# Attention by pair of heads ahead of two feed-forward nets: scores on quarters of the TensorE array, one transfer for queries and keys, softmax over several blocks at once, shared PSUM banks

## The chip, the cores and the metric

The kernel runs on one core of a Trainium2 chip. The metric is the device time of one execution in microseconds, the median of several runs. The profile is that of one execution, taken by the hardware profiler.

## What is computed

```
scores = scale * q @ k^T                                  # 4 batches, 8 heads, 576 tokens, 64 columns
mask_local   = (rel >= 0) & (rel < 32)                    # heads 0 to 3
mask_strided = (rel >= 0) & (pos_k % 32 == pos_q % 32)    # heads 4 to 7
attn = softmax(where(mask, scores, -1e9));  x = attn @ v  # x: [2304 tokens, 512]
h = x @ w_in;  x = (h * clip(h + 3, 0, 6) / 6) @ w_out    # 512 -> 2048 -> 512
h = x @ w_in2; out = (h * tanh(softplus(h))) @ w_out2
```

The weights come as doubles. Products of the two nets are made from split operands (a high and a low part of every number, three products in place of one); attention is in plain float32.

## The kernel before

**Attention.** A batch has four pairs of heads. A query sees few keys, so the 576 queries of a head are cut into nine blocks of 64, and a block is scored against the 96 keys (local heads) or 90 keys (strided heads) that it can see. A unit is three of the nine blocks of a pair, both heads: three units to a pair, twelve to a batch, 48 in all. `unit` scores a block of both heads with one product on the whole array: the stationary operand holds one head's 64 queries beside the other's, with zeros above and below, so that 128 rows of two heads come out (L415). VectorE scales, masks and takes the row's extremum with one fused instruction a block (L426), ScalarE takes the exponentials with their sums (L440, one instruction a block), VectorE adds 1e-9 and inverts (L450, L451), GpSimd multiplies (L444), TensorE transposes (L457), ScalarE or VectorE copies out of PSUM (L285, L287). `finish` makes the products with the values (L478), two units at a time from the second batch on, and splits the result into `xh` and `xl`.

**The nets.** Tokens go in five blocks (512, 512, 512, 256, 512). For each chunk of 128 of the 2048 hidden columns and each block there are four triples of products into the hidden chunk (from `xh`, `xl`) and four triples out of it (from `gh`, `gl`): L607, L608 and L609 are the three products of a triple. There are 1280 triples in all; a triple of 512 columns is three instructions of 128x512. A first-layer triple of the first token block needs the first batch's attention; later blocks need later batches.

**Order.** All engines' instructions are ordered ahead of time by a list planner (`Plan.run`) from estimated costs and due times, and stand in that order on the engines, which work strictly in it. SP issues all transfers, from one queue, in order as well. Numbers such as `UNIT` (an attention unit's time on TensorE), `START` and `EARLY_X` feed the planner, and `BANKS` says which of the eight PSUM banks each user may have. TensorE prints two records for every float32 product (it makes two passes) and one for each product of a triple and each transposition. In the first microseconds TensorE also multiplies zeros (L766) where it has nothing else to do.

Of the kernel before, what the change touches and what calls it, by code (L numbers as in the profile page):

```python
# [5 lines left out]
F32 = mybir.dt.float32  # L6
# [64 lines left out]
TWO_FROM = 1  # L71
#: Of mish: the seed a + b exp(-c w), and the step's square.
# [4 lines left out]
class Op:  # L77
    """Instructions of one engine that follow one another, what they wait for, and what they cost
    on the engines that could do them. VectorE and GpSimd read SBUF through a port that they share:
    lock names those engines on which the op holds it."""  # L80

    __slots__ = ("engine", "costs", "cost", "emit", "deps", "due", "bank", "frees", "start", "end", "left", "users", "rows", "lock")

    def __init__(self, costs, emit, deps, due, bank, frees, lock=""):
        self.engine, self.cost = min(costs.items(), key=lambda c: c[1])
        self.costs, self.emit, self.due = costs, emit, due
        self.deps = [d for d in deps if d is not None]
        self.bank, self.frees = bank, frees
# [13 lines left out]
class Plan:  # L102
    """Orders the instructions of all engines: each engine takes, of the instructions that can
    start first, the one that is due first."""

    #: From an instruction's end to the start of one that waits for it.
# [11 lines left out]
    def set_due(self):  # L118
        """What is due last before those that use it, back from the products."""
# [22 lines left out]
    def stream(self, t, op):  # L142
        """When TensorE, from t on, has done an op."""
# [10 lines left out]
    def fill(self, start, end, free_bank):  # L154
        """Products that nothing needs, on TensorE from start to end."""
# [14 lines left out]
    def run(self):  # L170
        """The instructions in the order of their starts."""
# [12 lines left out]
        while left:  # L184
            best = None
            for e, waiting in ready.items():
                for item in waiting:
                    r, op = item
                    if op.bank is not None and op.bank.n is None:
                        r = max(r, min(free_bank[n] for n in BANKS[op.bank.use]))  # L190
# [21 lines left out]
            if op.bank is not None and op.bank.n is None:  # L212
                op.bank.n = min(BANKS[op.bank.use], key=lambda n: free_bank[n])
                free_bank[op.bank.n] = 1e12
# [25 lines left out]
def copy_ns(n, psum=False):  # L240
    """Of a copy on either engine that may make it."""
# [3 lines left out]
def plain_ns(n):  # L245
    """Of two tensors' sum, difference or product."""
# [595 lines left out]
```

## Time and profile before

| | us |
|---|---|
| median of 3 runs | 907.26 (906.24 to 907.88) |
| profiled execution, span from first to last instruction | 909.7 |
| its own time apart from the span | not given; the span stands for it |
| TensorE busy | 901.1 (99%) |
| VectorE, ScalarE, GpSimd busy | 570.9, 543.7, 260.8 |
| bytes moved | 56.01 MB |

Read the page from its slices: a slice is 22.7 us, so attention (ended at 173.6 us on TensorE) fills the first seven or eight, and the rest is the nets.

### The profile page before, as it was taken

Reading aid. Unit: us, or ns where it says so; the run is one execution under the profiler, and the core shown is the slowest. Engines: PE = TensorE matmul, PEld = TensorE weight load, DVE = VectorE, ACT = ScalarE, POOL = GpSimd, SP = SyncE. Lnnn points to the kernel's source line nnn. Section 1 sums busy time; section 2 is a strip of 40 time slices with the busy share of each in tenths; the row PEclk is TensorE's granted clock in tenths of the full one; section 3 lists DMA queues with packets and bytes.
Section 4 is the critical chain, followed back from the end, with each engine's and each line's share of the span. In section 5 each row is a group of like instructions: output and inputs, shape, how many; then the busy total and the mean of one; then the engine's idle time right before and its main releaser. Section 6 shows DMA issues by size and latency. Waiting matters only on the chain.

```text
span 909.7 us, 13481 instructions
## 1 busy us (share of the span) xinstructions
PE 901.1 (99%) x4894; PEld 759.5 (83%) x4894; DVE 570.9 (63%) x1276; ACT 543.7 (60%) x1193; POOL 260.8 (29%) x240
## 2 busy tenths in 40 slices
PE   8999999999999999999999999999999999999998
PEld 8888888888888888888898888888888888888887
DVE  6787675588822258871237778646787787644454
ACT  6776867645322234332334878778887778666664
POOL 3223323232222222242443332222222222222222
PEclk9999999999999999999999999999999999999999
DMA  9944444022200002210002202100120110001111
GB/s 235 227 137 144 129 140 131 1 93 93 94 0 1 1 24 93 93 70 0 1 1 70 71 24 70 46 1 24 47 69 25 47 48 1 0 6 42 47 46 70
DMA packets 23146, 56.01 MB, mean 62 GB/s; under 512 B 2392, under 2 KB 9176, under 8 KB 23080
## 3 DMA queue, kind: packets, MB, share of 16 engines
q1 hardware_dynamic: 23080, 55.16, 19.7%
q8 instruction: 38, 0.62, 0.3%
q14 instruction: 28, 0.23, 0.1%
HBM read 50.43 MB, written 4.72 MB: 61 GB/s over the span
## 4 chain that ended last, share of the span: by engine, by line
PE 96%; DVE 1%; DMA 1%; SPq 1%; issue 0%; ACT 0%; DVEq 0%
PE bank L607 29%; PE bank L609 29%; PE bank L608 29%; PE bank L415 5%; PE bank L478 2%; PE bank L457 2%; DMA v<-in_qkv_dram 1%; SPq L380 0%; DVE e L426 0%; DVE wm L592 0%; SPq L388 0%; DVE y L739 0%; DVE sum L450 0%; SPq L383 0%; DVE t L618 0%
## 5 line engine op out<-in xcount | busy, mean ns | idle before, releaser
L701 POOL TENSOR_TENSOR gl<-t,gh 128x512 fp32r<-128x512 f32 (+1 forms) x160 | 197.8, 1237 | 534.6 <-ACT gh L285 485.4
L607 PE MATMUL bank<-xh,w 128*128 128x512 f32 (+1 forms) x640 | 240.0, 375 | 0.0
L607 PE MATMUL bank<-gh,w 128*128 128x512 f32 (+1 forms) x640 | 238.5, 373 | 0.0
L609 PE MATMUL bank<-xh,w 128*128 128x512 f32 (+1 forms) x640 | 237.5, 371 | 0.0
L608 PE MATMUL bank<-xl,w 128*128 128x512 f32 (+1 forms) x640 | 237.0, 370 | 0.0
L609 PE MATMUL bank<-gh,w 128*128 128x512 f32 (+1 forms) x640 | 237.0, 370 | 0.0
L608 PE MATMUL bank<-gl,w 128*128 128x512 f32 (+1 forms) x640 | 236.6, 370 | 0.0
L609 PEld LDWEIGHTS bank<-xh,w 128*128 128x128 f32 x640 | 120.7, 189 | 21.5
L607 PEld LDWEIGHTS bank<-xh,w 128*128 128x128 f32 x640 | 121.1, 189 | 20.4
L609 PEld LDWEIGHTS bank<-gh,w 128*128 128x128 f32 x640 | 120.4, 188 | 21.3
L608 PEld LDWEIGHTS bank<-xl,w 128*128 128x128 f32 x640 | 121.0, 189 | 20.5
L607 PEld LDWEIGHTS bank<-gh,w 128*128 128x128 f32 x640 | 120.6, 188 | 20.7
L608 PEld LDWEIGHTS bank<-gl,w 128*128 128x128 f32 x640 | 120.5, 188 | 20.6
L615 ACT ACTIVATE t<-bank 128x512 f32<-128x512 f32 (+1 forms) x80 | 44.4, 555 | 145.3 <-PE bank L609 143.6
L618 DVE SCALAR_TENSOR_TENSOR t<-t,bank 128x512 f32<-128x512 f32 (+1 forms) x80 | 50.6, 633 | 126.9 <-ACT t L615 126.6
L285 ACT CAST gh<-t 128x512 fp32r<-128x512 f32 (+1 forms) x160 | 91.3, 572 | 52.0 <-DVE t L618 27.6
L646 DVE SCALAR_TENSOR_TENSOR t<-t,seed 128x512 f32<-128x512 f32 (+1 forms) x80 | 60.8, 760 | 71.3 <-ACT seed L635 68.3
L651 DVE SCALAR_TENSOR_TENSOR t<-t,seed 128x512 f32<-128x512 f32 (+1 forms) x80 | 61.5, 770 | 48.0 <-ACT t L648 48.0
L639 ACT ACTIVATE t<-bank 128x512 f32<-128x512 f32 (+1 forms) x80 | 44.4, 555 | 60.4 <-PE bank L609 56.8
L648 ACT ACTIVATE t<-t,offset 128x512 f32<-128x512 f32 (+1 forms) x80 | 54.3, 679 | 23.2 <-DVE t L646 23.2
L739 DVE TENSOR_TENSOR y<-bank,y 128x512 f32<-128x512 f32 (+1 forms) x80 | 49.0, 634 | 21.8 <-PE bank L609 21.0
L444 POOL TENSOR_TENSOR e<-e,sum 128x288 f32<-128x288 f32 (+1 forms) x48 | 33.9, 711 | 89.9 <-DVE sum L451 47.2
(50 smaller groups left out, 1026.4 us busy)
## 6 DMA issues: line engine op xcount, KB each, us to landing
raw<-in_wts_dram SPq DMA_DIRECT2D x64, 512.0 KB, 3.5
k<-in_qkv_dram SPq DMA_DIRECT2D x15, 288.0 KB, 4.2
q<-in_qkv_dram SPq DMA_DIRECT2D x30, 144.0 KB, 4.4
out_dram<-y SPq DMA_DIRECT2D x16, 256.0 KB, 2.0
v<-in_qkv_dram SPq DMA_DIRECT2D x8, 432.0 KB, 4.7
v<-in_qkv_dram SPq DMA_DIRECT2D x7, 405.0 KB, 5.0
out_dram<-y SPq DMA_DIRECT2D x4, 128.0 KB, 1.8
mk_str<-in_masks_dram SPq DMA_DIRECT2D x1, 405.0 KB, 10.4
```

The costliest lines, as they stand in the source:

```text
L285: nc.scalar.copy(out, src)
L415: nc.tensor.matmul(banks[bank.n][:, j * LK:j * LK + nk], src.q[:, i].rearrange("p h (n j) -> p (h n) j", j=3)[:, :, j], src.k[:, k0:k0 + n ...
L607: nc.tensor.matmul(o, a[:, 1], high, start=first, stop=False)
L608: nc.tensor.matmul(o, a[:, 0], low, start=False, stop=False)
L609: nc.tensor.matmul(o, a[:, 0], high, start=False, stop=last)
L615: o = add("act", act_ns(n, True), lambda: nc.scalar.activation(t, h(), AF.Relu, bias=0.5, scale=1.0 / 6.0), [prod, free])
L618: lambda: nc.vector.scalar_tensor_tensor(t, t, 1.0, h(), ALU.min, ALU.mult), [o], frees=s.h,
L646: lambda: nc.vector.scalar_tensor_tensor(t, t, 4.0, seed(), ALU.add, ALU.mult), [o], lock=("dve",),
L648: o = add("act", act_ns(n), lambda: nc.scalar.activation(t, t, AF.Square, bias=offset, scale=scale), [o])
L651: lambda: nc.vector.scalar_tensor_tensor(t, t, more, seed(), ALU.add, ALU.mult), [o], lock=("dve",),
L701: lambda eng, gh=gh, gl=gl, t=t: engines[eng].tensor_tensor(gl, t, gh.bitcast(F32), ALU.subtract),
L739: lambda y=y, src=src: nc.vector.tensor_tensor(y(), src(), y(), ALU.add), [op, *before], due=due, frees=bank,
```

## The change

A unit becomes a whole pair. `attend` takes the place of `unit` and `finish`:

- **Scores.** A head's block is a product of its own on a quarter of the array: 64 rows of contraction (the head's columns) by 64 queries, 18 products to a pair, written to two banks, one for each head. No zeros stand beside the queries any more, so queries and keys come in one transfer of 128 x 1152 words, and values in one of all 128 rows (96 or 90 before).
- **Softmax.** Scores of a head are scaled and masked four blocks (two by two, one above the other) in one instruction, the ninth block in a second one; maxima are taken over four and over five block columns at once; sums, inverses and the multiplication go over four and five at once. The exponentials stay one instruction a block column, nine to a pair as before. The local mask is copied out four times on GpSimd at the start, the strided one comes in three smaller transfers.
- **Transpositions and values.** Nine transpositions to a pair, copied out in pieces of 4, 4 and 1; the values' products of eight blocks, then of the ninth.
- **Banks and plan.** Attention and the first layer's hidden chunks share banks 0 to 3; score, transposition and triple costs and the pace and due numbers of the planner are new.

```diff
-N_QKV, N_E, N_PT = 2, 4, 2
+N_QKV, N_E, N_PT = 2, 2, 2
...
-    "att": (2, 3),
+    "att": (0, 1, 2, 3),
...
-    "h0": (0, 1),
+    "h0": (0, 1, 2, 3),
...
-START, FIRST_PACE = 40000, 803
-UNIT = 800
+START, FIRST_PACE = 40000, 2409
+UNIT = 3000
...
-EARLY_W, EARLY_G, EARLY_X = 8224, 12000, 9101
+EARLY_W, EARLY_G, EARLY_X = 8224, 12000, 14000
...
+def mm3_ns(n):
+
+    return 3 * (n + 32) / 2.4
...
+        r.qk = add(
+            "dma", dma_ns(4 * P * 2 * S), lambda: nc.sync.dma_start(qk_t[n], qkv[b, p, :, :2 * S]), old.scores if old else [],
+        )
...
+        r.v_load = add(
+            "dma", dma_ns(4 * P * P * NB), lambda: nc.sync.dma_start(r.v, qkv[b, p, :, 2 * S:]), old.values if old else [],
+        )
...
+        def scores():
+            for n in range(NB):
+                for h in range(2):
+                    at = h if n == NB - 1 else n % 2
+                    nc.tensor.matmul(
+                        head(h)[at * QB:(at + 1) * QB, n // 2 * LK:n // 2 * LK + nk],
+                        src.q[h * D:(h + 1) * D, n // 3, :, n % 3],
+                        src.k[h * D:(h + 1) * D, first[n]:first[n] + nk],
+                        start=True,
+                        stop=True,
+                    )
...
+            nc.vector.scalar_tensor_tensor(
+                e[:, h * n:(h + 1) * n, :nk], x, 1.0 / INV_SCALE, mk_loc if local else mk_str[:, :n], ALU.mult, ALU.add
+            )
...
+        def most(s):
+            nc.vector.tensor_reduce(nmax[:, s], e[:, s, :nk], mybir.AxisListType.X, ALU.max, negate=True)
+
+        def exps(s):
+            for j in range(s.start, s.stop):
+                x = e[:, j, :nk]
+                nc.scalar.activation(x, x, AF.Exp, bias=nmax[:, j:j + 1], accum_out=total[:, j:j + 1])
...
+        s_op = add("pe", 36 * 44, scores, [src.qk, *e_free], bank=both)
...
-        s = add("pe", 640, scores, [*src.qk, e_free], bank=bank)
...
-                nc.tensor.matmul(
-                    banks[bank.n][:, j * LK:j * LK + nk],
-                    src.q[:, i].rearrange("p h (n j) -> p (h n) j", j=3)[:, :, j],
-                    src.k[:, k0:k0 + nk],
-                    start=True,
-                    stop=True,
-                )
```

**SP, the first transfers of the program** (`raw` are weights as doubles, `q`, `k`, `v` the operands of attention, `mk` and `mk_str` masks, `y` the memory in which the third pair's operands stand). Before:

```order
L558 DMA raw_91<-in_wts_dram 128x512
L383 DMA k_119<-in_qkv_dram 128x576
L380 DMA q_117<-in_qkv_dram 64x3x192 x2
L388 DMA mk<-in_masks_dram 128x320
L383 DMA k_120<-in_qkv_dram 128x576
L380 DMA q_118<-in_qkv_dram 64x3x192 x2
L392 DMA v_121<-in_qkv_dram 96x1152
L558 DMA raw_92<-in_wts_dram 128x512
L383 DMA y_77<-in_qkv_dram 128x576
L380 DMA y_77<-in_qkv_dram 64x3x192 x2
```

After:

```order
L392 DMA qk_118<-in_qkv_dram 128x1152
L372 DMA mk<-in_masks_dram 128x320
L392 DMA qk_119<-in_qkv_dram 128x1152
L392 DMA y_77<-in_qkv_dram 128x1152
L573 DMA raw_91<-in_wts_dram 128x512
L392 DMA qk_118<-in_qkv_dram 128x1152
L398 DMA v_120<-in_qkv_dram 128x1152
L380 DMA mk_str<-in_masks_dram 64x5x90
L380 DMA mk_str<-in_masks_dram 64x4x90
L380 DMA mk_str<-in_masks_dram 64x90
L398 DMA v_121<-in_qkv_dram 128x1152
L398 DMA y_78<-in_qkv_dram 128x1152
```

Four pairs' queries and keys and three pairs' values stand ahead of the second half chunk of weights now, where before that half chunk stood behind two pairs' queries and keys and one pair's values.

**TensorE, from the third product triple on**, where the start ends (`bank` are PSUM banks, `pt` the transposed weights of attention, `e` its weights, `w` decoded weights of the nets). Before, the part from the fourth pair's last units to the fourth and fifth triple:

```order
L607 MATMUL bank_62<-xh_71,w_79 128x512 [waits Activation_49]
L608 MATMUL bank_62<-xl_75,w_79 128x512 [waits DVE_49]
L609 MATMUL bank_62<-xh_71,w_79 128x512
L457 MATMUL bank_67<-mk,e_126 90x128 [waits Pool_49]
L457 MATMUL bank_67<-mk,e_126 90x128 x2
L478 MATMUL bank_63<-pt_135,v_121 64x64 [waits Activation_49]
L478 MATMUL bank_63<-pt_135,v_121 64x64 x5
L415 MATMUL bank_64<-k_119,q_117 128x96 [waits DMAHW3_49,DMAHW4_49,DMAHW2_49,DVE_49]
L415 MATMUL bank_64<-k_119,q_117 128x96 x2
L478 MATMUL bank_61<-pt_136,v_121 64x64 [waits Activation_49]
L478 MATMUL bank_61<-pt_136,v_121 64x64 x5
```

After, the fourth triple, and what stands between it and the fifth (18 rows of scores, of which the first two are shown):

```order
L623 MATMUL bank_63<-xl_76,w_79 128x512 [waits DVE_49]
L624 MATMUL bank_63<-xh_72,w_79 128x512
L479 MATMUL bank_62<-mk,e_122 96x128 [waits Pool_49]
L479 MATMUL bank_62<-mk,e_122 96x128 [waits Activation_49] x3
L479 MATMUL bank_61<-mk,e_122 96x128 [waits Pool_49]
L479 MATMUL bank_61<-mk,e_122 96x128 [waits Activation_49] x3
L479 MATMUL bank_63<-mk,e_122 96x128 [waits DVE_49]
L421 MATMUL bank_64<-qk_119 64x90 [waits DMAHW3_49,DVE_49]
L421 MATMUL bank_62<-qk_119 64x90 [waits Activation_49]
...
L498 MATMUL bank_61<-pt_128,v_121 64x64 [waits DMAHW2_49,Activation_49]
L498 MATMUL bank_61<-pt_128,v_121 64x64 x15
L622 MATMUL bank_66<-gh_103,w_80 128x512
```

Ahead of the fifth triple TensorE now waits for the queries and keys of the seventh pair (`qk_119`) and for the values of the fifth (`v_121`). Counted in the whole order, it has then 7 pairs of scores, 5 of transpositions and 5 of values behind it; before, it had 17 of 48 units of scores, 14 of transpositions and 12 of values. Behind the fifth triple there remain 31 units of scores, 34 of transpositions and 36 of values (in 24 groups) before, and 9 pairs of scores, 11 of transpositions and 11 of values (in 14 groups) now; 1276 triples either way.

## Rows read from the trace of the kernel before

**Rows 1.** The page, 40 slices of the span: TensorE's and the DMA engines' busy tenths.

```profile
PE   8999999999999999999999999999999999999998
...
DMA  9944444022200002210002202100120110001111
```

**Rows 2.** The page, the chain that ended last: shares by engine, then by line.

```profile
PE 96%; DVE 1%; DMA 1%; SPq 1%; issue 0%; ACT 0%; DVEq 0%
PE bank L607 29%; PE bank L609 29%; PE bank L608 29%; PE bank L415 5%; PE bank L478 2%; PE bank L457 2%; DMA v<-in_qkv_dram 1%; SPq L380 0%; DVE e L426 0%; DVE wm L592 0%; SPq L388 0%; DVE y L739 0%; DVE sum L450 0%; SPq L383 0%; DVE t L618 0%
```

**Rows 3.** Windows: length; busy of PE, PEld, DVE, ACT, POOL; clock; DMA share; GB/s.

```profile
0.00:12.00 12.00, 10.20 (x54) 9.94 (x55) 5.99 (x32) 6.02 (x21) 4.31 (x11) 1.00 0.83 247
12.00:24.00 12.00, 10.53 (x109) 9.95 (x108) 9.13 (x53) 8.55 (x37) 3.92 (x6) 1.00 1.07 220
24.00:36.00 12.00, 12.00 (x129) 10.88 (x129) 10.60 (x60) 9.63 (x41) 2.83 (x5) 1.00 1.03 234
36.00:46.00 10.00, 8.76 (x60) 7.52 (x59) 5.89 (x34) 6.80 (x29) 2.55 (x4) 0.75 0.74 211
46.00:174.00 128.00, 127.46 (x1000) 106.31 (x999) 86.88 (x361) 90.28 (x302) 39.34 (x45) 0.99 0.42 121
174.00:905.00 731.00, 731.00 (x3544) 613.98 (x3543) 450.94 (x736) 422.45 (x767) 207.84 (x170) 1.00 0.12 40
...
41.00:47.70 6.70, 6.70 (x34) 5.66 (x34) 4.18 (x21) 4.21 (x16) 0.86 (x2) 0.50 0.50 148
```

**Rows 4.** The chain cut to 46 to 174 us, shares by line.

```profile
by line: PE bank L415 25.0%; PE bank L607 16.5%; PE bank L609 15.3%; PE bank L608 15.0%; PE bank L478 10.9%; PE bank L457 9.2%; DVE e L426 1.2%; DVE t L618 1.0%; DVE sum L450 1.0%; issue 0.9%; DVE wm L592 0.9%; DVE wa L569 0.6%; DVE wa L578
```

**Rows 5.** The chain in order of time, pieces: start us, us, what (records).

```profile
32.19 2.06 PE bank L415 x12
34.26 0.85 PE bank L478 x24
...
96.08 0.33 PE bank L457 x3
97.90 0.23 PE bank L608
99.06 0.50 PE bank L478 x12
101.74 1.01 PE bank L415 x6
```

**Rows 6.** Groups by line and shape, weight loads: xcount, busy us, mean ns, idle.

```profile
L415 PEld LDWEIGHTS bank<-k,q 128*128 128x128 f32 x270 | 51.0, 262 | 5.2 <-DVE sum L451 1.4 <-DVE nmax L426 1.3 <-issue 0.9
L478 PEld LDWEIGHTS bank<-pt,v 96*64 96x64 f32 x288 | 9.7, 137 | 5.6 <-ACT e L440 2.7 <-issue 1.8 <-DVE sum L450 0.4
```

**Rows 7.** Timeline of TensorE, the fourth and the fifth product triple's first instruction.

```profile
44.09 0.77 PE L607 MATMUL bank<-xh,w 128*128 128x512 f32 x1
46.01 0.78 PE L607 MATMUL bank<-xh,w 128*128 128x512 f32 x1
```

**Rows 8.** DMA issues: xcount, KB each, median us from issue to landing.

```profile
k<-in_qkv_dram SPq DMA_DIRECT2D x15, 288.0 KB, 4.2
v<-in_qkv_dram SPq DMA_DIRECT2D x8, 432.0 KB, 4.7
mk_str<-in_masks_dram SPq DMA_DIRECT2D x1, 405.0 KB, 10.4
```

**Rows 9.** Groups by line and shape, the softmax and its nearest instructions.

```profile
L618 DVE SCALAR_TENSOR_TENSOR t<-t,bank 128x512 f32<-128x512 f32 x64 | 43.9, 686 | 95.0 <-ACT t L615 94.8
L440 ACT ACTIVATE e<-e,nmax 128x96 f32<-128x96 f32 x72 | 26.1, 365 | 5.4 <-DVE nmax L426 5.2
L444 POOL TENSOR_TENSOR e<-e,sum 128x288 f32<-128x288 f32 x24 | 17.6, 740 | 45.1 <-DVE sum L451 24.3 <-ACT e L440 11.3 <-ACT pt L285 4.0
L426 DVE CUSTOM_DVE_ANT_0 e<-bank,mk 128x96 f32<-128x96 f32 x72 | 14.8, 254 | 20.0 <-PE bank L415 19.0 <-PE bank L457 0.6 <-issue 0.2
L618 DVE SCALAR_TENSOR_TENSOR t<-t,bank 128x256 f32<-128x256 f32 x16 | 6.7, 422 | 31.9 <-ACT t L615 31.8
```

More of the change, by code (lines that the diff above doesn't have):

```diff
@@ L77 @@
 class Op:
-    __slots__ = ("engine", "costs", "cost", "emit", "deps", "due", "bank", "frees", "start", "end", "left", "users", "rows", "lock")
+    __slots__ = ("engine", "costs", "cost", "emit", "deps", "due", "banks", "frees", "start", "end", "left", "users", "rows", "lock")
     def __init__(self, costs, emit, deps, due, bank, frees, lock=""):
@@ L188, in run @@
                     r, op = item
-                    if op.bank is not None and op.bank.n is None:
-                        r = max(r, min(free_bank[n] for n in BANKS[op.bank.use]))
+                    if wanted := sum(k.n is None for k in op.banks):
+                        r = max(r, sorted(free_bank[n] for n in BANKS[op.banks[0].use])[wanted - 1])
                     at = {x: max(r, free[x], lock_free if x in op.lock else 0) for x in op.costs}
@@ L211, in run @@
                 lock_free = op.end
-            if op.bank is not None and op.bank.n is None:
-                op.bank.n = min(BANKS[op.bank.use], key=lambda n: free_bank[n])
-                free_bank[op.bank.n] = 1e12
+            for k in op.banks:
+                if k.n is None:
+                    k.n = min(BANKS[k.use], key=lambda n: free_bank[n])
+                    free_bank[k.n] = 1e12
             if op.frees is not None:
@@ L367, in load_pair @@
         n = 0 if k == 2 else 1 + (k if k < 2 else k - 1) % N_QKV
-        old = pair_ops.get({3: 0, 4: 1}.get(k, k - 2 if k > 4 else None))
-        r = pair_ops[k] = Record()
-        r.q, r.k, r.v = q_t[n], k_t[n], v_t[n]
-        r.scores, r.values, r.blocks = [], [], {}
-        if n not in q_zero:
-            q_zero[n] = [
-                add("pool", pool_ns(S / 2), lambda h=h: nc.gpsimd.memset(r.q[(1 - h) * D:(2 - h) * D, :, h], 0.0))
-                for h in range(2)
-            ]
-        free = old.scores if old else []
@@ L378, in load_pair @@
-        cost = dma_ns(4 * D * S)
-        r.qk = q_zero[n] + [
-            add("dma", cost, lambda h=h: nc.sync.dma_start(r.q[h * D:(h + 1) * D, :, h], qkv[b, p, h * D:(h + 1) * D, :S]), free)
+        old = pairs.get({3: 0, 4: 1}.get(k, k - 2 if k > 4 else None))
+        r = pairs[k] = Record()
+        r.q, r.k, r.v = qk_t[n][:, :S].rearrange("p (i n j) -> p i n j", i=3, j=3), qk_t[n][:, S:2 * S], v_t[n]
+        r.scores, r.values = [], []
+        r.qk = add(
+            "dma", dma_ns(4 * P * 2 * S), lambda: nc.sync.dma_start(qk_t[n], qkv[b, p, :, :2 * S]), old.scores if old else [],
+        )
@@ new lines, in load_pair, with attend, masked, normalize @@
+        local = p < NPAIR // 2
+        if local not in mk_load:
+            mk_load[local] = load_masks(local)
+        r.v_load = add(
+            "dma", dma_ns(4 * P * P * NB), lambda: nc.sync.dma_start(r.v, qkv[b, p, :, 2 * S:]), old.values if old else [],
+        )
+        return r
+    def attend(b, p):
+        src = load_pair(b, p)
+        kk = b * NPAIR + p
+        local = p < NPAIR // 2
+        nk = LK if local else SK
+        first = [max(0, QB * n - STRIDE) if local else min(S - SK, QB * n // NCLS * NCLS) for n in range(NB)]
+        e, nmax, total = e_t[kk % N_E], nmax_t[kk % N_E], sum_t[kk % N_E]
+        pt = pt_t[kk % N_PT]
+        use = "att" if b else "first"
+        e_free, pt_free = last_use.get(("e", kk - N_E), []), last_use.get(("pt", kk - N_PT), [])
+        both = [Bank(use), Bank(use)]
+        head = lambda h: banks[both[h].n]
+        def scores():
[9 more added lines that the diff above has]
+                    )
+        def masked(h):
+            n = NS - 1
+            rows = slice(h * QB, (h + 1) * QB)
+            x = head(h)[:, :n * LK].rearrange("p (s k) -> p s k", k=LK)[:, :, :nk]
+            nc.vector.scalar_tensor_tensor(
+                e[:, h * n:(h + 1) * n, :nk], x, 1.0 / INV_SCALE, mk_loc if local else mk_str[:, :n], ALU.mult, ALU.add
+            )
+            nc.vector.scalar_tensor_tensor(
+                e[rows, 2 * n, :nk], head(h)[rows, n * LK:n * LK + nk], 1.0 / INV_SCALE,
+                mk_loc[rows, 1] if local else mk_str[rows, n], ALU.mult, ALU.add,
+            )
+        def most(s):
[4 more added lines that the diff above has]
+                nc.scalar.activation(x, x, AF.Exp, bias=nmax[:, j:j + 1], accum_out=total[:, j:j + 1])
+        def normalize(eng, s):
+            x = e[:, s, :nk]
+            engines[eng].tensor_tensor(x, x, total[:, s].unsqueeze(2).to_broadcast([P, s.stop - s.start, nk]), ALU.mult)
+        n = NS - 1
+        s_op = add("pe", 36 * 44, scores, [src.qk, *e_free], bank=both)
+        src.scores.append(s_op)
+        load = mk_load[local]
+        masks_done = [
+            add("dve", dve_ns(n * nk * 1.1) + dve_ns(nk), lambda h=h: masked(h), [s_op, *load, *e_free], frees=both[h])
@@ L477, in values @@
+        last_use["e", kk] = t_ops
+        done = []
+        for blk, bank, col in ((range(2 * n), Bank(use), 0), (range(2 * n, NB), v_bank, P)):
+            nq = len(blk) * QB
+            def values(blk=blk, bank=bank, col=col):
+                for i, a in enumerate(blk):
                     for h in range(2):
+                        at = 2 * n * P + h * QB if a == NB - 1 else (h * n + a // 2) * P + a % 2 * QB
                         nc.tensor.matmul(
-                            banks[bank.n][h * D:(h + 1) * D, (3 * k + j) * QB:(3 * k + j + 1) * QB],
@@ L484, in values @@
                         )
-        av = add("pe", 450 * len(us) + 80, values, [*(o for *_, o in parts), src.v_load], bank=bank)
-        av.rows = nk / P
-        for u in us:
-            last_use["pt", u] = av
-        src.values.append(av)
-        def views():
-            o, x = banks[bank.n][:, :nq], [x[p][:, b * S:(b + 1) * S] for x in (xh, xl)]
-            if not local:
-                return [o] + [x[:, 3 * QB * first:][:, :nq] for x in x]
-            t = 3 * QB // STRIDE * first
-            x = [x.rearrange("p (r t) -> p t r", t=NCLS)[:, t:t + nq // STRIDE] for x in x]
-            return [o.rearrange("p (t r) -> p t r", r=STRIDE)] + x
@@ new lines, in attend, with views @@
+            av.rows = nk / P
+            last_use.setdefault(("pt", kk), []).append(av)
+            src.values.append(av)
+            def views(blk=blk, bank=bank, nq=nq, col=col):
+                o, x = banks[bank.n][:, col:col + nq], [x[p][:, b * S:(b + 1) * S] for x in (xh, xl)]
+                if not local:
+                    return [o] + [x[:, QB * blk[0]:][:, :nq] for x in x]
+                t = QB // STRIDE * blk[0]
+                x = [x.rearrange("p (r t) -> p t r", t=NCLS)[:, t:t + nq // STRIDE] for x in x]
+                return [o.rearrange("p (t r) -> p t r", r=STRIDE)] + x
@@ L527, in attention_then_two_ffns @@
+    attended = [op for ready in x_ready for ops in ready for op in ops]
     closing = add("act", 0, open_late, attended)
```

183 lines of the change are left out of this document (71 added, 112 removed).

## Prediction

> **What bounds the kernel now.** I read the slices of the page first: TensorE is busy from one end to the other, and the DMA engines are full for the first two slices alone [rows 1]. The chain that ended last says the same by line: 96% of it is TensorE, 29% for each product of a triple, and only 9% attention's own lines L415, L478 and L457 [rows 2]. So the time is the sum of what TensorE does, and a change counts by the TensorE time that it takes out, by the time at which the dense work starts, and by new gaps.
>
> Windows cut the span into three [rows 3]. Up to 46 us is the start: the first batch's attention, while transfers move at 211 to 247 GB/s with the DMA engines full, and TensorE waits for data. In it the clock falls to half: 0.50 granted from 41.0 to 47.7 us, that is 1.2 GHz of 2.4, after TensorE was idle for part of the time before (8.76 of 10 us busy in the window from 36 to 46). From 46 to 174 us three batches' attention lies between the triples, TensorE busy 127.46 of 128 us. After 174 us there are triples alone, which the change doesn't touch. The chain cut to the middle stretch gives 25.0% to the scores' line, 10.9% to values and 9.2% to transpositions [rows 4]: the scores cost 32.0 us of path. That is the term at stake.
>
> **The scores' old price.** A unit takes 1.01 us on the chain, six records; two in a row take 2.06 [rows 5]. I use 1.03 us (0.172 us a record). Behind the fifth triple, where the start ends, the order before has 31 units of scores: 31 x 1.03 = 31.9 us, which agrees with the 32.0 above. A record of 96 columns is not 0.172 us of streaming. Three transpositions of 128 columns take 0.33 us [rows 5], so 0.86 ns a column, and 96 columns 82 ns. The other 90 ns is the weight load of 128 strided columns, which isn't hidden: the loads of L415 fill 51.0 us for 270, 189 ns each, against a mean of 262, whereas those of L478 fill 9.7 us for 288, 34 ns each against a mean of 137 [rows 6], so these overlap almost wholly.
>
> **The new price.** A pair has 18 products of 64 x 64 x 96, 36 records. The trace of before shows no products on different halves of the rows at once. The nearest are the values, which alternate between the two halves of the columns: 24 records take 0.85 us and 12 take 0.50 [rows 5], so 29 ns a record and 0.15 us for entering. A record of 64 columns alone would stream 55 ns by the price above, so two go at once. At two at once, 96 columns make 82 ns, with the same 5% on top 87 ns for two records, and 18 x 87 ns = 1.57 us a pair. The load gives the same: 64 strided columns are half of 90 ns plus half of 82 ns, 86 ns, if two loads go at once. With the entry, 1.72 us. The bounds: below, 36 records at the densest spacing that the trace shows, 29 ns, 1.05 us and 1.20 with the entry; above, one after another with the load exposed, 45 + 82 = 127 ns each, 4.57 and 4.72 us. I take 1.72, nearest to the values' row, which shares the float32 passes and the half of the columns. 9 pairs behind the fifth triple: 15.5 us in place of 31.9, **-16.4 us**.
>
> The Trainium skill, "TensorEngine Tiling (Array Packing)", Key Properties, says that tiles load and multiply independently, which for four quarters means four at once; the trace agrees for two tiles of columns (29 ns a record against 55). By that rule a pair would take 9 x 87 ns + 0.15 = 0.93 us and the sum fall by another 7.1 us; it is the second case below. The same section says that a change of tiling mode drains the engine, which speaks against the change; the 0.15 us of entry is what the trace has of it, and if leaving costs as much, 9 x 0.15 = 1.4 us are lost.
>
> **Values and transpositions.** Their instructions are the same. Behind the fifth triple there are 36 units in 24 groups before, 12 x 0.85 + 12 x 0.50 = 16.2 us, and 11 pairs in 14 groups after, 396 x 0.029 + 14 x 0.15 = 13.6 us: -2.6 us. One unit of transpositions less, 0.33 us. Together **-2.9 us**: most of it is work that the start takes in.
>
> **The start.** The fifth triple starts at 46.01 us before [rows 7]. Ahead of it now stand the seventh pair's scores, and so its queries and keys. In SP's order there are, up to and with them, 7 x 0.590 MB of queries and keys, 5 x 0.590 of values (0.442 or 0.415 before), masks of 0.164 and 0.230 (0.415 before), and 4 x 0.524 of weights: 9.57 MB. At the rates of the windows 8.41 MB are there at 36 us, the rest 5 us later, at 41. Under this load a transfer lands late, the strided mask 10.4 us after its issue where others take 4.2 to 4.7 in the median [rows 8], since it shares the engines with those behind it; I allow 3 us, 44. Scores and 36 value records after it take 2.9 us. A second chain runs beside it, the fifth pair's softmax, whose transpositions stand ahead of the seventh pair's scores: 4 of 9 exponentials are 1.5 us and the multiplication of 480 columns 1.2 [rows 9], each half behind decoding work on VectorE. I take 48.5 us, **+2.5 us**, with 44 (nothing late) and 54 (scores, values and softmax one after the other, at half clock) as bounds. For the clock I add nothing: before has its 6.7 us at half as well [rows 3], and a second such stretch would cost what is done in it, half of it 3.4 us, which the bounds hold.
>
> **Gaps in the stretch with attention.** A pair's softmax is a longer chain with two buffers in place of four, and hidden chunks share banks 0 to 3 with attention. VectorE does nine fused instructions of 0.25 us a pair now; then four, two of 384 columns (0.55 us, between 0.42 for 256 and 0.69 for 512) and two of 96 (0.25), and two maxima (0.5 to 0.6) [rows 9]: 2.3 us become 2.7. Over 11 pairs VectorE has 91 us in place of 86.9, ScalarE 90.3 or a little less, in a stretch of about 110 us in place of 128 [rows 3]: 83% in place of 68 to 71%. Neither is the bound, but TensorE works in order and meets a late engine oftener. What hides a late exponential is the triples between a pair's scores and its transpositions. I take **+3 us**, bounds 0 and 8. GpSimd (39.3 of 128 us) has room, and the two SP issues a pair saved hide behind full DMA engines. One transfer for queries and keys moves the same bytes: no gain but in the start's order.
>
> **Sum.** -16.4 - 2.9 + 2.5 + 3 = -13.8 us. The profiled execution has 909.7 us, 2.4 over the median of 907.26; 909.7 - 13.8 = 895.9 in its terms, and **893.5 us** as a median.
>
> **The rivals.**
> - *Four at once.* 0.93 to 1.20 us a pair, 4.7 to 7.1 us less: 886 to 889. For it: quarters share neither rows nor columns. Against: a product's two passes need the same quarter, so in order only neighbours overlap. 0.10.
> - *Another engine holds the stretch.* The softmax chain comes late and gaps are 8 us, the fifth triple starts at 52: 893.5 + 5 + 3.5 = 902. For it: 83% on two engines that work in order. Against: TensorE has no gap at 71%. 0.17.
> - *Nothing changes.* Strided loads go one after another, 86 ns each: 3.1 us and 0.15 a pair, 29.3 us for nine, 13.8 more than I take: 907. For it: the exposed load. 0.06.
> - *Slower.* On halves of the rows neither loads nor products overlap, 4.72 us a pair, 42.5 us for nine, +27: 920. It decides from 3.26 us a pair, 86 ns a record after the entry, where the 13.8 us are used up. Against: the values' overlap. 0.05.
>
> **How the numbers follow.** My forecast has 0.62, with 885 to 901 as its own range (1.5 to 2.3 us a pair is -2 to +5; start and gaps do the rest). A measurement of this kernel can tell some 0.2%, 1.8 us. The range of 884 to 905 takes in the forecast, most of four at once, and the late engine; it leaves out the slower case, the unchanged one and the ends of the others, under 0.2. Faster: 0.62 + 0.10 + 0.15 of the late engine + 0.02 = 0.89. Same: 0.03 + 0.02 = 0.05. Slower: 0.05 + 0.01 = 0.06.
>
> **What would show it.** In the profile after, 36 records of scores take 1.5 to 1.8 us from first to last, their starts about 44 ns apart on average; the last values stand at 155 to 160 us in place of 173.6; the fifth triple at 46 to 51; the part after attention is unchanged at 0.23 us a product. The forecast is wrong if the scores' starts are 85 ns or more apart, if TensorE shows waits for ScalarE or VectorE of more than 8 us in the stretch, or if the clock stays at half far beyond the start.

## The result and the profile after

The changed kernel takes **892.5 us** (median of 4 runs, 890.12 to 894.95) where the kernel before takes 907.2 on the same chip (906.24 to 907.88): a ratio of 0.9836, 95% interval 0.9822 to 0.985, 14.7 us faster. The forecast was 893.5. The profiled execution has a span of 890.2 us and a time of 892.15.

The page of the changed kernel, busy tenths in 40 slices of 22.3 us (against [rows 1]):

```profile
PE   9699999999999999999999999999999999999998
...
PEclk9899999999999999999999999999999999999999
DMA  8655650323000022300002022000221100000111
```

TensorE is no longer full in the second slice, and its granted clock falls there. The windows of the changed kernel, with the columns of [rows 3]:

```profile
0.00:12.00 12.00, 10.20 (x107) 9.39 (x108) 5.56 (x17) 4.61 (x20) 0.97 (x6) 1.00 0.85 315
12.00:24.00 12.00, 9.95 (x165) 9.01 (x164) 9.73 (x24) 8.69 (x42) 3.66 (x4) 1.00 0.80 260
24.00:36.00 12.00, 10.90 (x150) 8.60 (x152) 10.02 (x28) 9.38 (x35) 3.82 (x4) 0.72 0.66 228
36.00:46.00 10.00, 5.58 (x79) 3.89 (x78) 9.88 (x23) 7.80 (x27) 3.35 (x3) 0.93 0.63 224
46.00:157.00 111.00, 107.75 (x1187) 84.86 (x1184) 91.78 (x226) 90.20 (x314) 34.75 (x34) 0.99 0.47 149
...
24.00:31.00 7.00, 5.90 (x46) 4.42 (x47) 6.24 (x18) 5.66 (x26) 3.06 (x4) 0.51 0.73 267
44.60:48.00 3.40, 3.40 (x51) 2.81 (x53) 3.37 (x6) 2.35 (x10) 1.26 (x1) 0.50 0.28 114
```

Three things differ from before. The first 12 us move 315 GB/s with the DMA engines at a share of 0.85, where before moved 247 at 0.83, and the next 12 us move 260 at 0.80 where it moved 220 with them full (257 and 262 in a second execution of before, below). From 36 to 46 us TensorE is busy 5.58 of 10 us and VectorE 9.88. The clock is at half, 1.2 GHz, twice: from 24.0 to 31.0 and from 44.6 to 48.0 us. The chain of the changed kernel, cut to 46 to 157 us (against [rows 4]):

```profile
by line: PE bank L622 14.0%; PE bank L624 11.9%; PE bank L623 11.8%; ACT e L448 11.8%; PE bank L498 6.8%; PE bank L479 6.5%; PE bank L421 4.8%; DVE e L434 3.8%; ACT xh L290 3.3%; ACT pt L290 3.0%; DVE xl L526 2.7%; issue 2.5%; DVE nmax L443
```

The scores' line (L421 now) has fallen from 25.0% to 4.8%, and the exponentials on ScalarE (L448) have 11.8%. Pieces of the timelines of the changed kernel on TensorE, VectorE and GpSimd (start, length in us, what; in brackets the idle time before and who ended it):

```profile
37.47 1.14 PE L421 MATMUL bank<-qk 64*64 64x96 f32 x36
...
39.10 0.40 PE L624 MATMUL bank<-xh,w 128*128 128x512 f32 x1
42.08 0.64 PE L479 MATMUL bank<-mk,e 128*96 128x128 f32 x4 [2.58 <-POOL e L452]
44.56 1.30 PE L479 MATMUL bank<-mk,e 128*96 128x128 f32 x5 [1.84 <-POOL e L452]
45.79 1.78 PE L421 MATMUL bank<-qk 64*64 64x90 f32 x36
47.50 1.48 PE L498 MATMUL bank<-pt,v 96*64 96x64 f32 x36
48.91 0.50 PE L622 MATMUL bank<-gh,w 128*128 128x512 f32 x1
...
150.30 1.27 PE L498 MATMUL bank<-pt,v 90*64 90x64 f32 x36
...
40.93 1.09 POOL L452 TENSOR_TENSOR e<-e,sum 128x384 f32<-128x384 f32 x1 [9.18 <-ACT e L448]
...
44.66 1.26 POOL L716 TENSOR_TENSOR gl<-t,gh 128x512 fp32r<-128x512 f32 x1 [0.16 <-ACT gh L290]
...
35.24 0.68 DVE L593 SCALAR_TENSOR_TENSOR wa<-raw,wa 128x512 uint32<-128x512 uint32 x1
...
37.17 0.42 DVE L599 TENSOR_SCALAR wa<-wa 128x512 uint32<-128x512 uint32 x1
...
41.26 1.31 DVE L593 SCALAR_TENSOR_TENSOR wa<-raw,wa 128x512 uint32<-128x512 uint32 x1
...
44.71 1.50 DVE L599 TENSOR_SCALAR wa<-wa 128x512 uint32<-128x512 uint32 x1
```

A pair's 36 score records take 1.14 us from the first start to the last end. One record is 0.25 long in the trace, so the starts lie (1.14 - 0.25) / 35 = 25 ns apart. The fifth triple starts at 48.91 us, after TensorE stood idle for the fifth pair's transpositions (2.58 and 1.84 us); the last values stand at 150.30, to 151.6.

What TensorE waited for in the changed kernel up to 50 us (total, times, longest), from the view of waits:

```profile
PE bank L479 <- POOL e L452: 5.0, 3, 2.6
PE bank L498 <- ACT pt L290: 2.6, 1, 2.6
PE bank L781 <- DVE offset L776: 1.2, 1, 1.2
PE bank L421 <- DMA qk<-in_qkv_dram: 0.5, 1, 0.5
```

7.6 us are the softmax (its last step on GpSimd, L452, and the copy of its transpositions, L290); transfers of queries and keys held it for 0.5.

### The profile page after: what moved, and what is told of

Same layout as the page of the kernel before. It is cut to its first block, busy times and chain, and to the rows that moved or that the text cites. A ratio compares the mean times of both kernels' runs of the same rounds, so it can differ in the third digit from the quotient of the medians.

```text
span 890.2 us, 13727 instructions
## 1 busy us (share of the span) xinstructions
PE 874.2 (98%) x5206; PEld 728.3 (82%) x5206; DVE 576.5 (65%) x1046; ACT 541.3 (61%) x1192; POOL 255.3 (29%) x219
## 4 chain that ended last, share of the span: by engine, by line
PE 91%; DVE 4%; ACT 3%; DMA 1%; issue 1%; POOL 0%; SPq 0%; ACTq 0%; POOLq 0%; DVEq 0%
PE bank L622 29%; PE bank L624 29%; PE bank L623 29%; ACT e L448 2%; PE bank L479 1%; PE bank L421 1%; PE bank L498 1%; DVE e L434 1%; PE bank L781 1%; DMA qk<-in_qkv_dram 1%; DVE nmax L443 0%; DVE xl L526 0%; ACT xh L290 0%; DMA raw<-in_wts_dram 0%; ACT pt L290 0%
## 5 line engine op out<-in xcount | busy, mean ns | idle before, releaser
L716 POOL TENSOR_TENSOR gl<-t,gh 128x512 fp32r<-128x512 f32 (+1 forms) x160 | 200.1, 1252 | 546.3 <-ACT gh L290 509.3
L633 DVE SCALAR_TENSOR_TENSOR t<-t,bank 128x512 f32<-128x512 f32 (+1 forms) x80 | 50.6, 633 | 140.6 <-ACT t L630 140.0
L290 ACT CAST gh<-t 128x512 fp32r<-128x512 f32 (+1 forms) x160 | 91.5, 572 | 54.4 <-DVE t L633 33.7
L661 DVE SCALAR_TENSOR_TENSOR t<-t,seed 128x512 f32<-128x512 f32 (+1 forms) x80 | 70.9, 887 | 62.7 <-ACT seed L650 61.6
L666 DVE SCALAR_TENSOR_TENSOR t<-t,seed 128x512 f32<-128x512 f32 (+1 forms) x80 | 58.8, 736 | 43.9 <-ACT t L663 43.9
L448 ACT ACTIVATE e<-e,nmax 128x96 f32<-128x96 f32 (+1 forms) x144 | 51.7, 363 | 12.6 <-DVE nmax L443 12.1
```

The source lines that it names most:

```text
L290: nc.scalar.copy(out, src)
L448: nc.scalar.activation(x, x, AF.Exp, bias=nmax[:, j:j + 1], accum_out=total[:, j:j + 1])
L633: lambda: nc.vector.scalar_tensor_tensor(t, t, 1.0, h(), ALU.min, ALU.mult), [o], frees=s.h,
L661: lambda: nc.vector.scalar_tensor_tensor(t, t, 4.0, seed(), ALU.add, ALU.mult), [o], lock=("dve",),
L666: lambda: nc.vector.scalar_tensor_tensor(t, t, more, seed(), ALU.add, ALU.mult), [o], lock=("dve",),
L716: lambda eng, gh=gh, gl=gl, t=t: engines[eng].tensor_tensor(gl, t, gh.bitcast(F32), ALU.subtract),
```

## The experiments

Theory A: scores of different quarters go at once, as many as stand next to each other, and this term is larger than forecast; the start gives a part of it back. The rivals: small products are short by themselves, whatever stands next to them (B), or a chain beside TensorE sets the time. For the start, the causes tried are transfers (D), the clock (C), the work on VectorE (V), the two softmax buffers (B in that run) and the order (O, P).

**Score order: one_head, one_side, one_quarter.** The same 18 products a pair, in other orders:

```diff
-            for n in range(NB):
-                for h in range(2):
+            for n, h in [(n, h) for h in range(2) for n in range(NB)]:                            # one_head
+            for n, h in [(n, h) for o in range(2) for n in range(NB) for h in range(2)
+                         if (h if n == NB - 1 else n % 2) == o]:                                  # one_side
+            for n, h in [(n, h) for h in range(2) for o in range(2) for n in range(NB)
+                         if (h if n == NB - 1 else n % 2) == o]:                                  # one_quarter
```

> The changed kernel with the same 18 score products a pair in another order: all of the first head, then all of the second, so neighbours use one half of the rows and alternate between the halves of the columns. Theory A (products of different quarters go at once, as many as follow one another in different quarters): two at a time, 36 records in 1.5 to 1.8 us in place of 1.15, and about 9 x 0.5 = 4 to 6 us more in all (897 to 898). Rival B (a 64 x 64 product of 96 columns is short by itself, whatever its neighbours): still 1.15 us, 892.5 within 1.8.

> The changed kernel with the score products ordered by their half of the columns, the two heads (halves of the rows) alternating. Theory A: if halves of the rows go at once as halves of the columns do, 1.5 to 1.8 us a pair, 897 to 898, as in the order by heads; if they do not, 86 to 127 ns a record, 3.1 to 4.6 us a pair, and 18 to 31 us more. Rival B: 1.15 us a pair, 892.5 within 1.8.

> The changed kernel with the score products ordered quarter by quarter, nine in a row on each. Theory A: one product at a time, 86 to 127 ns a record, 3.1 to 4.6 us a pair, 18 to 31 us more than 892.5, so that the whole gain is gone. Rival B: 1.15 us a pair, 892.5 within 1.8. A third theory (the time is set by a chain beside TensorE, so that a longer TensorE step is taken up by its gaps): scores of 3 us or more a pair, but the total rises by less than half of that.

The timelines of one_head, one_side and one_quarter, one pair of the same place in each:

```profile
95.09 1.74 PE L421 MATMUL bank<-qk 64*64 64x90 f32 x36
```

```profile
95.46 1.73 PE L421 MATMUL bank<-qk 64*64 64x90 f32 x36
```

```profile
100.04 2.58 PE L421 MATMUL bank<-qk 64*64 64x90 f32 x36
```

On average over a pair, the starts lie 25 ns apart with all four quarters in turn, (1.74 - 0.25) / 35 = 43 with two, whether these share rows or columns, and (2.58 - 0.25) / 35 = 67 with one after another. B falls. What lies under these averages shows in 0.6 us from within a pair, of the changed kernel, of one_head and of one_quarter:

```profile
68.63 0.61 PE L421 MATMUL bank<-qk 64*64 64x96 f32 x20
```

```profile
95.25 0.61 PE L421 MATMUL bank<-qk 64*64 64x90 f32 x10
```

```profile
100.20 0.60 PE L421 MATMUL bank<-qk 64*64 64x90 f32 x5
```

In the same time 20, 10 and 5 records start: five sets of four, of two and of one. From set to set it is (0.61 - 0.25) / 4 = 90 or (0.60 - 0.25) / 4 = 88 ns in all three, with 96 columns as with 90. A quarter took its next record after some 88 ns, whatever the others did. So the 67 ns are not the step of one quarter alone. In one_quarter a quarter gets five, four, four and five products in a row (not nine), and the first record of each, 0.32 us long in the trace where the others have 0.25, stands at 100.04, 100.65, 101.08 and 101.51 us, though ten records 88 ns apart take 0.79 us from first to last start and eight take 0.62: neighbouring quarters overlap for part of their time. That is why its pair takes 2.58 us and not the 3.1 to 4.6 that was expected.

The times: 898.71 us (ratio 0.9904, 0.9879 to 0.993), 896.27 (0.9876, 0.9861 to 0.9891) and 911.27 (1.0038, 1.0015 to 1.006). Behind the fifth triple there are nine pairs: 9 x 0.60 = 5.4 us and 9 x 1.44 = 13 us are to be expected, the spans have risen by 4.3, 4.6 and 14.4. So most or all of a longer score step goes into the time. The third theory, a chain beside TensorE by which less than half would go into it, falls. With one quarter after another the whole gain is gone. The profile of one_quarter is of the fastest of its ten runs (906.34; the slowest took 915.26); by the medians it lost 18.8 us, and no profile shows where the other 4 to 6 went.

**The kernel before once more: before_again.** No edit.

> The kernel before once more, for its span and its start. The profile of before has 909.7 us from its first instruction to its last, 2.4 over the median of the times, while the changed kernel's times lie 1.9 above their spans. Theory A: that execution was some 4 us longer than usual, in its start; here the span is 905 to 906 and the fifth triple stands at 41 to 44 us in place of 46.0, with the part after 174 us unchanged. Rival: the span of before is usually 909 to 910, and its start is as it was, 46.0 within 0.5.

Its windows and a piece of its TensorE timeline:

```profile
0.00:12.00 12.00, 9.73 (x48) 9.57 (x49) 5.81 (x29) 6.02 (x21) 4.13 (x11) 0.86 0.87 257
12.00:24.00 12.00, 12.00 (x122) 11.68 (x122) 9.70 (x57) 8.84 (x40) 4.13 (x7) 1.00 1.06 262
24.00:36.00 12.00, 12.00 (x129) 10.88 (x128) 10.88 (x60) 10.13 (x45) 3.41 (x5) 1.00 0.87 225
...
41.00:47.70 6.70, 6.08 (x51) 4.67 (x51) 5.96 (x18) 6.25 (x20) 2.95 (x4) 1.00 0.55 172
```

```profile
42.00 0.47 PE L607 MATMUL bank<-xh,w 128*128 128x512 f32 x1
```

The span is 905.4 us (time 907.23), the fifth triple starts at 42.00 us in place of 46.01 [rows 7], and there is no half clock where the first profile has one [rows 3]: TensorE is full from 12 to 36 us. The profile that the prediction was made from shows an execution 4.3 us longer than this one, 4.0 of them in its start. On TensorE the part after the last values is the same 732.5 us in both. Such an execution is rare but not alone: of ten runs of before_again one took 911.43 us, the others 905.88 to 907.50.

**The start: loads_before, fill_48, no_clamp, no_three.** Four causes, one by one:

```diff
-        r.qk = add("dma", ..., lambda: nc.sync.dma_start(qk_t[n], qkv[b, p, :, :2 * S]), ...)
+        r.qk = [add("dma", ..., lambda h=h: nc.sync.dma_start(qk_t[n][h * D:(h + 1) * D, :S],
+                    qkv[b, p, h * D:(h + 1) * D, :S]), free) for h in range(2)] + [add("dma", ...,
+                    lambda: nc.sync.dma_start(qk_t[n][:, S:2 * S], qkv[b, p, :, S:2 * S]), free)]
-        ... nc.sync.dma_start(r.v, qkv[b, p, :, 2 * S:])
+        ... nc.sync.dma_start(r.v[:LK if local else SK],
+                    qkv[b, p, :LK if local else SK, 2 * S:])                       # loads_before: both
-FILL, FILL_UNTIL = 128, 20974
+FILL, FILL_UNTIL = 128, 48000                                                      # fill_48
-            lambda: nc.vector.tensor_scalar(a, a, TINY, HUGE, ALU.max, ALU.min), [o], lock=("dve",),
+            lambda: None, [o], lock=("dve",),                                      # no_clamp, no_three
-            lambda: nc.vector.tensor_scalar(ai, ai, 3, 0x3FFFF000, ALU.logical_shift_left, ALU.bitwise_and),
+            lambda: None,                                                          # no_three
-            lambda: nc.vector.tensor_scalar(ai, ai, 0xFF800000, None, ALU.bitwise_and), [o], lock=("dve",),
+            lambda: None, [o], lock=("dve",),                                      # no_three
```

> The changed kernel with the transfers cut as before: the queries in two transfers of 64 partitions, the keys in a third, the values on 96 or 90 partitions. Theory V: the transfers land a little later (the seventh pair's queries and keys at 37 to 39 us in place of 36.0), but VectorE holds the start: fifth triple within 1 us of 48.9, 892.5 within 1.8. Rival D (the one transfer and the full rows brought the rate of 315 and 260 GB/s, and the start lives by it): windows at 210 to 250 GB/s with the DMA engines full, fifth triple 2 to 5 us later, 895 to 898.

> The changed kernel with products of zeros planned into TensorE's gaps until 48 us in place of 21 (29 more of 128 columns; the plan's order shifts with them). Theory C (the half clock from 24.1 to 30.9 and 44.6 to 48.0 us costs TensorE, which is on the path there): the granted clock stays at 1.00 in at least one of the two, fifth triple 1 to 3 us earlier, 889.5 to 891.5. Theory V: TensorE waits for VectorE and the softmax anyway; the fifth triple within 0.7 us, 892.5 within 1.8, whether the clock stays up or not.

> The changed kernel without the clamp of the decoded weights (one VectorE instruction of 0.42 us in each half chunk of weights; weights out of float32's range would come out otherwise). The order of all the rest is as it was, to the end of the start. Theory V (the start is held by VectorE, 9.88 of 10 us busy from 36 to 46, and by the softmax that waits in its order): some 7 of them stand ahead of the fifth triple, which comes 2 to 4 us earlier than 48.9, and the time falls by 2 to 5 us to 888 to 890. Rival T (VectorE is full but TensorE would have waited for transfers or ScalarE all the same): fifth triple within 0.7 us, 892.5 within 1.8.

> The changed kernel without three of the seven VectorE instructions that decode each half chunk of weights (the clamp, the shift of the exponent, the power of two; some 0.34 us each in a row of them), in the same order; the weights that it decodes are not the right ones. The clamp alone left the fifth triple at 48.3 us and the total where it was. Theory V (in the start a pair's softmax stands in VectorE's order between pieces of decoding, 4.5 us of them in the chain of waits from 31 to 42 us): some 7 x 1 us less on VectorE ahead of the fifth triple, which comes at 44 to 46.5; the time falls by 2 to 5 us, to 887.5 to 890.5. Rival L (the softmax's own steps, one after the other with a wait between each, hold TensorE): fifth triple at 47.5 or later, 892.5 within 1.8.

| | time, us | ratio, 95% interval | fifth triple at | span |
|---|---|---|---|---|
| the changed kernel | 892.50 | 0.9822 to 0.985 | 48.91 | 890.2 |
| loads_before | 894.23 | 0.9846 to 0.9876 | 49.95 | 891.6 |
| fill_48 | 892.78 | 0.9822 to 0.9854 | 45.07 | 888.3 |
| no_clamp | 891.46 | 0.9812 to 0.9842 | 48.33 | 890.0 |
| no_three | 891.52 | 0.9822 to 0.9855 | 47.78 | 888.0 |

None is told apart from the changed kernel by its time. With the transfers as before the windows of loads_before read

```profile
0.00:12.00 12.00, 9.76 (x93) 8.43 (x94) 4.59 (x14) 3.99 (x16) 0.97 (x6) 1.00 0.85 225
12.00:24.00 12.00, 11.75 (x179) 10.81 (x177) 8.09 (x22) 7.52 (x35) 3.63 (x4) 1.00 1.04 268
```

against 315 GB/s at the same DMA share, and yet the fifth triple is only 1.0 us later: D's rate came in the first window alone, and its price for the start did not come. In fill_48 the granted clock is 1.00 in every window and the fifth triple comes 3.8 us sooner, but behind it TensorE then has 5.6 us of idle time up to the last values in place of 3.2, and the median is where it was. V falls too: no_three takes three of seven decoding instructions from VectorE, and TensorE waits for the softmax in its start as long as it does with them. Its waits up to 50 us:

```profile
PE bank L479 <- POOL e L452: 5.1, 3, 2.5
PE bank L498 <- ACT pt L290: 2.6, 1, 2.6
```

**Buffers and order: e3_early, plan_before, tuned, tuned_short.** A third softmax buffer for the first six pairs (the first sums, which use its memory, then wait for twelve pairs in place of eight); the planner's two old numbers; eight numbers of the planner fitted to the new kernel, the true price of a pair's scores among them; the same without the longer stretch of products of zeros.

```diff
-        e, nmax, total = e_t[kk % N_E], nmax_t[kk % N_E], sum_t[kk % N_E]
+        ke = kk % 3 if kk < 6 else kk % 2                                          # e3_early; the third
+        e, nmax, total = e_t[ke], nmax_t[ke], sum_t[ke]                            # lies in sums[0]
```

```diff
-UNIT = 3000
+UNIT = 2400                                                                        # plan_before
-EARLY_W, EARLY_G, EARLY_X = 8224, 12000, 14000
+EARLY_W, EARLY_G, EARLY_X = 8224, 12000, 9101                                      # plan_before
```

```diff
-START, FIRST_PACE = 40000, 2409
+START, FIRST_PACE = 40000, 3300                                                    # tuned: all of these
-UNIT = 3000
-HALF_PACE = 6263
-EARLY_W, EARLY_G, EARLY_X = 8224, 12000, 14000
+UNIT = 1600
+HALF_PACE = 6500
+EARLY_W, EARLY_G, EARLY_X = 7700, 10200, 8300
-FILL, FILL_UNTIL = 128, 20974
+FILL, FILL_UNTIL = 128, 60000                                                      # not in tuned_short
-        s_op = add("pe", 36 * 44, scores, [src.qk, *e_free], bank=both)
+        s_op = add("pe", 36 * 31, scores, [src.qk, *e_free], bank=both)
```

> The changed kernel with a third buffer for the softmax of the first six pairs (it stands in memory that the first sums take later), so that scores need not wait for the transpositions of the pair two ahead. Theory B (two buffers in place of four hold the start): TensorE's idle time ahead of the fifth triple falls from 8.2 to 5 us or less, the time by 2 to 4 us, 888.5 to 890.5. Theory V: the masks and maxima wait for VectorE all the same: 892.5 within 1.8.

> The changed kernel with two of the planner's numbers as they were: the attention of a batch due 9.1 us ahead of its first product in place of 14, and 2.4 us of TensorE a pair in place of 3. The first batch is not touched by the second number much; attention comes later in the order. Theory P (the order holds what the shorter scores gave, since with a pair's longer softmax a late start of it stops TensorE): more waits for ScalarE and VectorE between 50 and 150 us, 3 to 8 us slower, 895 to 900. Rival: fewer pairs stand ahead of the fifth triple, so the start ends 3 to 6 us sooner and the sum stays, 892.5 within 1.8, or falls to 888 to 890.

> The changed kernel with the planner's numbers fitted to it: a pair's scores at 1.12 us in place of 1.58 (1.14 was measured), the attention due 8.3 us ahead of its products, 1.6 us of TensorE a pair, other lead times for weights and activations, products of zeros until 60 us. Theory O (what the quarters gave and the start took back is a question of the order; TensorE has 11.4 us of idle time up to the last values, and 10 us at half clock): half of it is regained, 885 to 889, beyond both kernels. Rival: what one place gains another loses, as in the order with the old lead times (fifth triple 7.5 us earlier, total -1.5): 890 to 892.5.

> The kernel with the fitted planner's numbers (883.4 us, TensorE without a gap and at the full clock in the start), but with products of zeros only until 21 us, as in the changed kernel; the order shifts a little with them. Theory O (the order of the work, not the products of zeros, gave the 9 us back): 884 to 887, a start with 1 to 3 us of idle time. Rival C (the gaps are short but the clock falls to half in the start again, 7 us or more, and with it the gain): 887.5 to 891, and the runs lie 2 to 5 us apart as those of the changed kernel do, where the fitted one's lie within 0.3.

| | time, us | ratio, 95% interval | runs | TensorE idle to the last values |
|---|---|---|---|---|
| the changed kernel | 892.50 | 0.9822 to 0.985 | 890.1 to 895.0 | 11.4 |
| e3_early | 891.38 | 0.9804 to 0.9855 | 889.3 to 893.7 | 11.1 |
| plan_before | 890.96 | 0.9798 to 0.9835 | 888.4 to 891.6 | 9.0 |
| tuned_short | 885.75 | 0.9736 to 0.9774 | 885.1 to 885.9 | 5.8 |
| tuned | **883.44** | 0.9727 to 0.9756 | 883.4 to 883.6 | 1.3 |

(The idle time is worked out from the records of TensorE, each gap between the end of all earlier ones and the next start.) The third buffer alone stays unclear: its fifth triple is at 41.63 us, but idle time behind it takes the place of that ahead of it. The two old numbers move the fifth triple to 41.41 us with two pairs fewer ahead of it, and the time by 1.5 us at most; P, which expected 895 to 900, falls. The fitted numbers give 9.1 us, with the fifth triple at 37.82 us and six pairs of scores ahead of it. The windows of tuned:

```profile
12.00:24.00 12.00, 11.90 (x175) 10.74 (x175) 11.16 (x31) 10.20 (x45) 3.94 (x4) 1.00 0.91 310
24.00:36.00 12.00, 12.00 (x196) 9.84 (x196) 11.85 (x35) 11.38 (x48) 3.37 (x4) 1.00 0.80 274
...
46.00:157.00 111.00, 110.70 (x1221) 89.81 (x1220) 92.47 (x225) 92.54 (x315) 38.28 (x37) 1.00 0.45 150
```

and of tuned_short:

```profile
24.00:36.00 12.00, 10.39 (x173) 8.05 (x171) 11.18 (x34) 10.61 (x45) 3.38 (x4) 0.86 0.75 253
```

From 24 to 36 us VectorE is busy 11.85 of 12 us, and TensorE has no gap all the same: what it needs comes in time. Without the longer stretch of products of zeros 6.8 of the 9.1 us stay, so most of it is the order; 2.3 us more come with the products of zeros, a full clock and the order that goes with them. Which of the other numbers does it was not tried.

## Why the prediction was right

The total was right, and in part by luck: two of its terms, the scores and the start, were mis-sized and offset each other. That TensorE's time sets the total, and that scores on quarters shorten it by overlapping, is borne out. Against the profile that it was made from, the span fell by 19.5 us, where the sum had 13.8.

- **Scores: -16.4 forecast, -20.9 found.** The step that failed is "so two go at once", carried over from the values. Four do: the 87 ns that the prediction gave to two records are what a set of four took (88 to 90). Behind the fifth triple the starts of 186 records fill 31.48 us before (31.9 in the prediction), those of 324 records 10.61 after (15.5). A pair takes 1.14 us, inside the bound of 1.05 to 1.20. The price for two, 1.72 us, is what one_head and one_side measured (1.74). The upper bound, 127 ns a record one after another, added the load (45) to the columns (82) and was too high: on one quarter a record follows after 88 ns, so load and columns overlap there too. The prediction had two reasons for its 87, the columns and the loads; as 90 and 96 columns have the same step, and it is half of the 172 ns that a record with 128 loaded columns took before, the loads of 64 fit better. This is argued, for no run changed the load alone. The old price, read as 82 of columns and 90 of load not hidden, would then be the load alone.
- **Four quarters.** The Trainium skill, "TensorEngine Tiling (Array Packing)", Key Properties, says that tiles load and multiply independently, and by that rule the prediction priced a second case at 0.93 us a pair. The trace agrees: one, two or four quarters, a set of records every 88 to 90 ns. The objection to this case, that in order only neighbours overlap, was too strict: the quarters of one_quarter begin before those ahead of them are done. Up to the next product's start a pair took 10.61 / 9 = 1.18 us, within the 0.93 to 1.20 of this rival. Its time of 886 to 889 did not come, since the start took more.
- **Values and transpositions: -2.9 forecast, -3.6 found** (16.54 to 13.63 us, and 10.06 to 9.39).
- **Start: +2.5 forecast, +2.9 found in the two profiles, +6.9 against before_again.** "The fifth triple starts at 46.01 us before" is true of one execution only; 42.00 is the place in the other. The 48.5 us were nearly met (48.91), for another reason than the one given: the seventh pair's transfer was not late, for TensorE waited 0.5 us in all for queries and keys, and the DMA engines were at 0.63. The second chain that the prediction named, the fifth pair's softmax, held it. A whole pair's scores, masks, maxima, exponentials, sums, multiplication and transpositions now follow one another, and the order had too little for TensorE in between: it idles 8.2 us ahead of the fifth triple, where before_again has 1.1 and tuned, in another order, 0.1. "For the clock I add nothing" leaned on the half clock of one execution: the changed kernel has 10.4 us at half, before_again none in 41 to 47.7. What these cost in the total is not shown, as fill_48 has none of them and the same median.
- **Gaps: +3 forecast, some +2 found.** Per 512-column product the start-to-start time rises from 260 to 269 ns between the fifth triple and the last values, (269 - 260) x 252 = 2.3 us. Whether the two buffers or the shared banks make these gaps was not tried apart. The last values stood at 151.6 us, sooner than the 155 to 160 forecast, because the scores were cheaper.
- **From span to median.** The sum was made against 909.7 us and lowered by 2.4. Times lie 1.7 to 2.0 above their spans in 12 of the 13 profiles taken here (907.23 and 905.4, 892.15 and 890.2; 3.3 in e3_early), so that profile was most likely of an execution some 4.3 us above the usual. Against before_again the span fell by 15.2: -20.9 - 3.6 + 2.3 + 6.9 = -15.3. So 4.5 us more from the scores went to a start that cost 4.4 more than forecast.
- **The late engine**, rival two, was half right: ScalarE and GpSimd do hold TensorE, but in the start and by the order. Its 8 us of gaps in the stretch did not come. In the nets nothing changed (0.23 us a product in both).

## What to carry to other kernels

When small products are packed on parts of the array, write neighbours in the program for different parts, and price them by the set: here up to four records for different parts took the time of one. When one engine's step gets shorter and another's chain longer, fit the order of the work again: here it was worth 9 us, more than half as much as the change itself. Before a sum is built on one profile, take a second one, and ask whether the start it shows is the usual one.

## What the runs showed of the hardware

- Halves of the rows overlap as well as halves of the columns (1.73 and 1.74 us a pair). Within a pair, two quarters in turn gave twice and four gave four times the records of one (10 and 20 against 5 in 0.6 us). Over a whole pair, with its first step and its last record, that became 1.74 and 1.14 us.
- One transfer of 128 rows of 4608 bytes for queries and keys, and values on all 128 rows, moved 315 GB/s in the first 12 us; cut as before, 225 GB/s at the same DMA share of 0.85. In the next 12 us it was 260 and 268. The two cuts were not taken apart.
- VectorE's decoding steps L593 and L599 take 0.68 and 0.42 us alone, and 1.31 and 1.50 beside an instruction of GpSimd (rows at 41.26 and 44.71 above): L599 ends at 46.21, 0.29 us after GpSimd's L716 at 45.92, as if it had stood still for most of that instruction. The Trainium skill, "SBUF — State Buffer", Terms, says that the two engines' shared port is held for a whole instruction and the loser fully blocks; these rows agree.
- From run to run the changed kernel spreads by 4.8 us (890.12 to 894.95) and tuned by 0.2 (883.36 to 883.60). A start with idle time at half clock does not settle it: fill_48, at full clock, spreads by 3.3 (890.09 to 893.42), and one_side by 0.7 (895.96 to 896.67) with 7.2 us idle ahead of its fifth triple and the clock at half from 43.8 to 50.6 us.
